# Two-expert attention kernel: block 0's softmax weights in PSUM, the first weights in halves on two load queues, the last copy in two, and a new issue order

## The chip, the cores and the metric

The kernel runs on one core of one Trainium2 chip. TensorE (PE, with its weight loads as PEld), VectorE (DVE), ScalarE (ACT) and GpSimd (POOL) work side by side, and SyncE (SP) issues DMAs and forwards semaphores. The metric is device microseconds of one execution, the median of repeated runs; lower is better.

## The reference, cut to what matters

```python
x_unf = x_pad[:, idx, :]                     # 2 x 4096 tokens, 7 taps, 192 = 8 heads x 24
w = softmax(weight_gen)                      # over the 7 taps, per head and token
x = einsum('bshk,bskhg->bshg', w, x_unf)     # attention
h = x @ w1_in;  g = h / (1 + exp(-h));  x = g @ w1_out            # expert 1, d_ff 2048
h = x @ w2_in;  g = P(h) / (Q(h) + 1e-6);  out = g @ w2_out       # expert 2
# P is a cubic, Q = 1 + |b0| |h| + |b1| h^2; all in float32
```

## The kernel before, in words

The 8192 tokens are cut into 16 blocks of 512 (4 tokens on each of 128 partitions). For each block the kernel computes the attention, turns the result so that features lie on partitions, and runs expert 1 and then expert 2, each in 8 units of 256 hidden features. Every float32 product is made of a high and a low part (`xh`, `xl`; `wa` high, low; `wb`; `g1h`, `g1l`; `g2h`, `g2l`), and TensorE works as two row groups of 64 rows that run side by side. All 9,728 products of 512 columns go through line 808. Eight PSUM areas are used: banks A to D (`h`, the turned tiles, decoded weights) and the accumulators of the two experts.

Nothing is scheduled at run time. `ORDER` is a list of some 3,960 names, written by a search outside the kernel, and each engine issues its instructions in the order in which the names stand there. A name is an operation, a unit and a block: `M2.0` is operation `M` of column 2 in block 0. A letter behind a colon is the buffer or bank taken, `@1` the second engine of the operation's choice, `^` and `^^` a load of the ACT function table, `<2` or `>2` a shift of the two row groups against each other. The names that matter here:

- `s0l`, `s0m`, `s0d`, `s0e`, `s0t`, `s0n`: load of weight_gen for block 0, maximum, subtraction, exponential, sum and reciprocal, and normalisation; `s1` is that of block 1, `s2` to `s5` of the rest.
- `X.b`, `Z.0`: loads of x. `Mj`, `mj`: the products of x and weights for 4 and 3 taps (768 and 576 elements); `pj`, `rj`, `aj`: the additions that leave 576, 384 and 192 of them.
- `q0B0l0`, `q0A0l1`: loads of the halves of an input weight (expert 0, piece B or A, half 0 or 1), `q0O1l0` of an output weight. Each half of B and A of the first expert comes in two DMAs of 64 partitions. Weights lie in HBM with 64 bits a number; `a` (ACT) and `4` (DVE) make a float32 of each half in a PSUM bank, `h` the high part, `x` the low part.
- `W0.0`, `W1.0`: transposes that only keep TensorE busy; `WT.0`, `T.b`: the attention turned; `XH`, `XL`: its high and low part.
- `Au`, `Ku` (expert 1) and `Bu`, `Qu` (expert 2): the products into an `h` bank. `S`, `H`, `L`: SiLU, high and low part; `U`, `V`, `u`, `w`, `Y`, `N`, `G`, `g`, `h`, `l`: the rational function and its parts. `C`, `E`, `I`, `F` and `D`, `P`, `J`, `R`: products into the accumulators. `EC`, `EM`, `EA`: the turn from expert 1 to 2; `FC`, `FT`, `FR`, `FE`, `FA`, `O`: the way out.

An `h` bank is free for its next tenant when `L` (line 923) or `w` (line 973) has read it. The first expert's first unit needs `XH`, `XL`, the weight A of its columns and the weight B.

Of the kernel before, what the change touches and what calls it, by code (L numbers as in the profile page):

```python
# [21 lines left out]
P = 128  # L22
# [28 lines left out]
    S4.0 H4.0:e r2.1 L4.0:t F4.0>2 M1.1:p q1B040:B q0O3h q1B0a1 q0O3x S6.0 A7.0:D>2 q1O0l1:i C2.0>2 q1O1l1:u
    q1O1l0:d r3.1@1 q1A0a0 H6.0:h q1B041 p1.1 q1B0h1 q1A0a1 K7.0 E4.0 S7.0 H7.0:v E5.0 E3.0 C4.0 M0.1:a L6.0:q
    C6.0<2 q1A040:A C7.0<4 p0.1 q1A041 q1B0x1 q1A1l0:c r0.1@1 a0.1:j q1A1l1:m L7.0:r q1O0a0 r1.1@1 a3.1@1 q1O040:D
    q1B0h0 a1.1 q1B0x0 q1O0a1 a2.1 q1A0h F6.0 q1O041 q1A0x q1O0h q1O0x q1O1a0 I6.0 T.1:B q1O140:A s3l:o E7.0 E6.0
    TR.1 XH0.1:q q1O1a1 F7.0 XL0.1:s q1O141 I7.0 I4.0>2 q1A1a0 EC.0:g q1O1h q1A140:B q1O1x A2.1:D q1A1a1 q1A141
    q1O2l1:w K2.1 S2.1 s3m H2.1:c EM.0 L2.1:n q1O2l0:t A1.1:A K1.1 q1A1h q1O3l1:d q1O2a1 S1.1 EA.0 XH1.0:h H1.1:p
    X.2 A0.1:D K0.1 S0.1 H0.1:a q1A1x XL1.0:i s3d@1 q1O2a0 L1.1:x s2n@1 L0.1:g s2s A3.1:B K3.1 S3.1 H3.1:l B0.0:C
    q1O240:A q1O241 B5.0:D q1O2h q1O3a1 L3.1:y Q0.0 V0.0:e q1O2x Q5.0 E1.1:B C3.1 V5.0:b C1.1<2 U5.0:w AW.2 B3.0:A<4
    U0.0:v Y0.0 Y5.0 m1.2:t M1.2:u I2.1<4 F1.1<1 q1O3l0:r Q3.0<1 M0.2:m ^^N0.0 U3.0:j F0.1<1 q1O3a0 V3.0:k m2.2:x
    u5.0 u0.0 w0.0 w5.0 I0.1<1 I1.1>1 B2.0:C>3 q1O340:D u3.0 m0.2:p q1O341 p0.2@1 F2.1>3 F3.1>3 w3.0 Q2.0>3 C0.1>3  # L60
# [1076 lines left out]
```

## Time and profile before

| | |
|---|---|
| median of 3 runs | 1193.26 us (1193.02 to 1193.70) |
| profiled execution | 1195.1 us, of which 1193.3 us lie between its first and last instruction |
| TensorE clock granted | 0.998 of full speed over the span |
| busy | PE 98%, DVE 91%, ACT 88%, POOL 43% |
| DMA | 45.42 MB |

The profile is of one execution. The page has the busy times, the span in slices and the groups of instructions; the trace answers for single stretches (windows, timeline), for waits and for the chain of work that ended last. TensorE's instructions overlap, so its busy share alone doesn't tell whether it ran at its full rate; the number of matmuls in a window does.

### The profile page before, as it was taken

What the parts mean: (1) busy time and instruction counts of PE and PEld (TensorE: products, weight loads), DVE (VectorE), ACT (ScalarE), POOL (GpSimd) and SP (SyncE); (2) the same over time, 40 slices, a digit from 0 to 9 for tenths busy, and PEclk for the clock granted to TensorE, in tenths of its full rate; (3) what the DMA queues carried; (4) which work ended last, traced back from release to release, by engine and by line L of the source; (5) the groups of instructions that cost most, each with busy time, mean ns of one, the idle gap of its engine ahead of it and who ended that gap; (6) DMA issues with size and microseconds to landing.
All of it is one profiled execution on the core that took longest, in us unless ns stands there. A gap on an engine that the chain in (4) does not pass through costs nothing.

```text
span 1193.3 us, 24919 instructions
## 1 busy us (share of the span) xinstructions
PE 1164.3 (98%) x10332; PEld 1072.2 (90%) x10332; DVE 1091.2 (91%) x1016; ACT 1049.3 (88%) x1023; POOL 518.1 (43%) x340
## 2 busy tenths in 40 slices
...
DMA packets 17753, 45.42 MB, mean 38 GB/s; under 512 B 2412, under 2 KB 9194, under 8 KB 17640
## 3 DMA queue, kind: packets, MB, share of 16 engines
...
q14 instruction: 32, 0.26, 0.1%
...
## 4 chain that ended last, share of the span: by engine, by line
PE 84%; DVE 5%; ACT 4%; issue 2%; SPq 0%; DVEq 0%; ACTq 0%
PE acc L808 44%; PE h L808 39%; DVE y L979 1%; ACT h L915 1%; DVE g1l L923 1%; ACT g1h L919 1%; PE to L1028 1%; PE tp L821 1%; DVE t L970 1%; DVE t L990 0%; DVE t L973 0%; DVE g2l L1000 0%; ACT L1102 0%; ACT y L964 0%; ACT t L960 0%
## 5 line engine op out<-in xcount | busy, mean ns | idle before, releaser
L808 PE MATMUL h<-xh,wa 64*128 64x512 f32 x2048 | 433.2, 393 | 6.6 <-DVE t L973 2.7
L808 PEld LDWEIGHTS h<-xh,wa 64*128 64x128 f32 x2048 | 274.7, 184 | 37.2 <-issue 4.9
L808 PE MATMUL h<-xh,wb 64*128 64x512 f32 x1024 | 293.5, 388 | 0.0
L808 PE MATMUL h<-xl,wa 64*128 64x512 f32 x1024 | 293.2, 388 | 0.0
L808 PE MATMUL acc<-g1h,wo 64*128 64x512 f32 x1536 | 286.1, 391 | 0.0
L808 PE MATMUL acc<-g2h,wo 64*128 64x512 f32 x1536 | 282.4, 390 | 0.0
L1000 POOL TENSOR_TENSOR g2l<-t,g2h 128x1024 fp32r<-128x1024 f32 x73 | 188.7, 2594 | 167.5 <-ACT g2h L464 55.0
L808 PEld LDWEIGHTS acc<-g1h,wo 64*128 64x128 f32 x1536 | 209.1, 184 | 11.5 <-ACT g1h L919 0.5
L808 PEld LDWEIGHTS acc<-g2h,wo 64*128 64x128 f32 x1536 | 210.1, 184 | 9.9 <-SPq L404 0.2
L808 PE MATMUL acc<-g2l,wo 64*128 64x512 f32 x1024 | 203.6, 391 | 1.6 <-DVE xl L842 1.5
L808 PE MATMUL acc<-g1l,wo 64*128 64x512 f32 x1024 | 202.9, 391 | 0.6 <-DVE g1l L923 0.4
L741 POOL TENSOR_TENSOR pr<-xw,aw 128x576 f32<-128x576 f32 (+1 forms) x76 | 116.7, 1549 | 172.9 <-PE acc L808 53.8
L979 DVE SCALAR_TENSOR_TENSOR y<-y,b_sb 128x1024 f32<-128x1024 f32 x128 | 177.0, 1389 | 10.4 <-ACT y L964 10.0
L923 DVE TENSOR_TENSOR g1l<-h,g1h 128x1024 fp32r<-128x1024 f32 x128 | 155.4, 1219 | 28.5 <-ACT g1h L919 19.4
L990 DVE SCALAR_TENSOR_TENSOR t<-t,a_sb,y 128x1024 f32<-128x1024 f32 x128 | 173.2, 1363 | 8.4 <-ACT y L987 7.7
L970 DVE TENSOR_TENSOR t<-t,h 128x1024 f32<-128x1024 f32 x128 | 155.1, 1214 | 16.6 <-ACT t L960 8.2
L915 ACT ACTIVATE h<-h 128x1024 f32<-128x1024 f32 x128 | 129.6, 1013 | 44.4 <-PE h L808 42.4
L960 ACT ACTIVATE t<-h,a_sb 128x1024 f32<-128x1024 f32 x128 | 153.7, 1204 | 16.0 <-PE h L808 13.2
L973 DVE SCALAR_TENSOR_TENSOR t<-t,a_sb,h 128x1024 f32<-128x1024 f32 x128 | 163.5, 1279 | 3.9 <-ACT y L964 0.4
L964 ACT ACTIVATE y<-h,b_sb 128x1024 f32<-128x1024 f32 x128 | 141.9, 1113 | 27.7 <-PE h L808 20.5
L808 PEld LDWEIGHTS h<-xl,wa 64*128 64x128 f32 x1024 | 151.1, 184 | 7.4 <-DVE xl L842 0.3
L808 PEld LDWEIGHTS h<-xh,wb 64*128 64x128 f32 x1024 | 150.9, 184 | 7.1
...
## 6 DMA issues: line engine op xcount, KB each, us to landing
...
```

What stands on the lines that cost most here:

```text
L741: e.tensor_tensor(out=p.rearrange("p k (h g) -> p k h g", g=G), in0=st[xw][:, j + k0:j + k0 + n, :].rearrange("p k (h g) -> p k h g", g=G) ...
L808: return pe.matmul(out=out, lhsT=w, rhs=x, start=start, stop=stop)
L821: return lambda: pe.transpose(out=st[tp][:, a, j * P + r * DL:j * P + (r + 1) * DL], in_=columns(a, j, r), identity=ident[HALF[r], HALF[r]],)
L915: act.activation(out=st[hb], in_=st[hb], func=AF.Silu)
L923: dve.tensor_tensor(out=t, in0=st[hb], in1=st[gh].bitcast(F32), op=ALU.subtract)
L960: act.activation(out=q, in_=st[hb], func=AF.Identity, scale=a_sb[:, 3:4], bias=a_sb[:, 2:3])
L964: act.activation(out=q, in_=st[hb], func=AF.Abs, scale=b_sb[:, 1:2])
L970: dve.tensor_tensor(out=st[t], in0=st[t], in1=flat(), op=ALU.mult)
L973: dve.scalar_tensor_tensor(out=st[t], in0=st[t], scalar=a_sb[:, 1:2], in1=flat(), op0=ALU.add, op1=ALU.mult)
L979: dve.scalar_tensor_tensor(out=st[y], in0=st[y], scalar=b_sb[:, 0:1], in1=st[y], op0=ALU.add, op1=ALU.mult)
L990: dve.scalar_tensor_tensor(out=st[t], in0=st[t], scalar=a_sb[:, 0:1], in1=st[y], op0=ALU.add, op1=ALU.mult)
L1000: e.tensor_tensor(out=q, in0=st[t], in1=st[gh].bitcast(F32), op=ALU.subtract)
```

## The change

Four things are changed. Block 0's normalised attention weights are copied by ACT into PSUM bank D (`cw`), and the products of its columns 0 to 2 read them there, on DVE; their last two additions (`r`, `a`) become one reduction over four (`fold`). The first piece of weight A gets its high and low parts in halves of 512 columns (`h0`, `x0`, `h1`, `x1`), and units 0 and 1 ask only for the first half; the second DMA of each half of this piece and of the first B is issued from ACT's queue in place of SP's. The last block's copy out of the accumulator is in two halves, one on ACT and one on DVE. And the whole `ORDER` is a new one: of its 240 lines none is kept, and of them the first and the last are shown.

```diff
--- before
+++ after
 ORDER = """
-    s0l cz:f s0m X.0 q0B0l0:h q0B0l1:x Z.0 s0d ^^s0e s0t s0n@1 M2.0@1:a M1.0@1:l q0B0a0 q0B040:B M0.0@1:q q0B0a1
-    q0B041 q0B0h0 m2.0@1:h m0.0@1:r M3.0@1:u m3.0@1:w q0B0h1 m1.0@1:e p2.0 p0.0 r2.0 p1.0 q0A0l0:b q0A0a0 cn
-    q0A040:C W0.0:A r0.0 r1.0 cl q0A0l1:s q0A0a1 q0A041 p3.0 a0.0@1:g s1l q0O0l0:n q0O0a0 ca r3.0@1 a1.0 q0B0x0 a3.0
-    a2.0 q0A0h q0A0x q0O040:D q0B0x1 s2l:k q0O0l1:d q0O1l0:t q0O0a1 q0O1l1:v WT.0 W1.0:B s1m q0O041 q0A1l0:h q0O1a0
-    q0A1l1:e s2m s1d@1 XH0.0:r XL0.0:y cr s2d@1 q0O140:C q0O1a1 q0O0h q0O0x q0O141 s1e s1t q0O1h@1 s2e X.1 q0O1x
-    A0.0 A1.0:A q0A1a0 K0.0 ^S0.0 H0.0:l L0.0:t q0O2l0:c A2.0:D K1.0 S1.0 H1.0:q s1n@1 L1.0:w K2.0 I0.0:C q0O2l1:x
+    s0l s0m s0d X.0 ^^s0e s0t s0n cw:D cz:f q0B0l0:i M2.0:g M0.0:b q0B0a0 q0B040:B M1.0:l q0B0l1:q cn Z.0 q0B0a1
+    q0B041 q0A0l1:p q0O0l1:r m3.0:q s1l q0A0l0:n q0B0h0 m0.0:w m1.0:h m2.0:o p0.0@1 M3.0:x q0B0x0 a0.0:a p1.0
+    q0O3l1:v s1m p3.0@1 q0B0h1 q0A0a0 W0.0:A q0A0a1 q0O1l0:u a1.0 q0O0l0:s p2.0 r3.0@1 cl a2.0 q0O1l1:e q0A040:C
+    a3.0 q0A1l1:d q0A1l0:b X.1 q0A0h0 ca q0B0x1 s1d@1 q0O0a0 s1e q0A041 q0O0a1 q0O040:D q0O2l0:h WT.0 XH0.0:l q0A0x0
+    q0O041 W1.0:B XL0.0:j q0A0h1 A0.0 K0.0 q0A0x1 q0O1a0 q0O0h q0O0x q1B0l0:t A1.0:A K1.0 q0O1a1 q0O140:C A2.0:D
 ...
-    P4.15 FR.14 R4.15 J4.15 FC.15:u FT.15:D FE.14@1 FA.14 O.14 FR.15 FE1.15 FA1.15 O1.15 FE0.15 FA0.15 O0.15
+    P6.15 P5.15 h4.15@1:p P3.15 l4.15:a D7.15 J7.15 J4.15 R7.15>2 R4.15 FR.14 P7.15 P4.15 D4.15 FE.14@1 FA.14 O.14
+    FC0.15:p FC1.15@1 FT.15:D FR.15 FE0.15 FA0.15 FE1.15@1 FA1.15 O0.15 O1.15
 """
```

```diff
                 f = slice(4 * n * q + 1, 4 * n * (q + 1))
+                queues = (sp, sp if m or c else act)
                 if k == "A" and m:
                     sp.dma_start(out=t[:, 0:4 * n - 1], in_=w_in[m][0:P, f])
...
                     for h in range(2):
-                        sp.dma_start(out=t[R[h], 0:4 * n - 1], in_=w_in[m][h * P:h * P + DL, f])
+                        queues[h].dma_start(out=t[R[h], 0:4 * n - 1], in_=w_in[m][h * P:h * P + DL, f])
                 elif k == "B":
                     for h in range(2):
                         f = slice(4 * n * (i + 2 * h) + 1, 4 * n * (i + 2 * h + 1))
-                        sp.dma_start(out=t[R[h], 0:4 * n - 1], in_=w_in[m][P if m else DL:D if m else P, f])
+                        queues[h].dma_start(out=t[R[h], 0:4 * n - 1], in_=w_in[m][P if m else DL:D if m else P, f])
                 else:
                     sp.dma_start(
...

-        def hi(e):
-            w, a, _ = halves()
-            if e is act:
-                act.activation(out=a, in_=w, func=AF.Copy, scale=256.0)
-            else:
-                dve.tensor_scalar(out=a, in0=w, scalar1=256.0, scalar2=None, op0=ALU.mult)
+        def hi(i=None):
+            q = slice(None) if i is None else slice(512 * i, 512 * (i + 1))
+
+            def run(e):
+                w, a, _ = halves()
+                w, a = w[:, q], a[:, q]
+                if e is act:
+                    act.activation(out=a, in_=w, func=AF.Copy, scale=256.0)
+                else:
+                    dve.tensor_scalar(out=a, in0=w, scalar1=256.0, scalar2=None, op0=ALU.mult)
+            return run
+
+        def lo_half(i):
+
+            def run(e):
+                w, a, b = halves()
+                q = slice(512 * i, 512 * (i + 1))
+                less(b[:, q], w[:, q], a[:, q])
+            return run

         def less(out, w, a):
...
             return
-        plan.op(name + "h", 0, "ACT DVE", hi, rd=full, wr=wt)
+        if k == "A" and (m, c) == (0, 0):
+            for i in range(2):
+                wt = [("W", m, k, c, i)]
+                plan.op(f"{name}h{i}", 0, "ACT DVE", hi(i), rd=[full[i], dt[0]], wr=wt)
+                plan.op(f"{name}x{i}", 0, "DVE", lo_half(i), rd=[full[i], dt[0], *wt], wr=wt)
+            return
+        plan.op(name + "h", 0, "ACT DVE", hi(), rd=full, wr=wt)
         plan.op(name + "x", 0, "DVE", lo, rd=[*full, *wt], wr=wt)

...

+        wp = ("h", "w", b)
+
         def weight(j):
-            return st["aw", b][:, j * HK:(j + 1) * HK].rearrange("p (h k) -> p k h", k=K)
+            t = st["aw", b] if b or j == JB - 1 else st[wp].rearrange("p a c -> p (a c)")
+            return t[:, j * HK:(j + 1) * HK].rearrange("p (h k) -> p k h", k=K)
+
+        def copy_w(e):
+            st[wp] = t = bank(wp)
+            act.activation(out=t[:, 0, 0:JB * HK], in_=st["aw", b][:, 0:JB * HK], func=AF.Copy)
+
+        if b == 0:
+            plan.op("cw", b, "ACT", copy_w, rd=[wt], wr=[(*wp, 0)])

         for j in range(JB):
             halves = [(*pr, j, 0), (*pr, j, 1)]
+            near = b == 0 and j < JB - 1

             def mul(i, j=j, halves=halves):
...

+            def fold(e, j=j, halves=halves):
+                if ao not in st:
+                    st[ao] = new(ao, [P, JB, D])
+                dve.tensor_reduce(
+                    out=st[ao][:, j], in_=st[halves[0]].rearrange("p k d -> p d k"), axis=AX.X, op=ALU.add
+                )
+
             pt, qt = [(*halves[0], 0)], [(*halves[1], 0)]
-            plan.op(f"M{j}", b, "POOL DVE", mul(0), rd=[*(xt if j == JB - 1 else xt[:1]), wt], wr=pt)
-            plan.op(f"m{j}", b, "POOL DVE", mul(1), rd=[*xt, wt], wr=qt)
+            who, w = ("DVE", (*wp, 0)) if near else ("POOL DVE", wt)
+            plan.op(f"M{j}", b, who, mul(0), rd=[*(xt if j == JB - 1 else xt[:1]), w], wr=pt)
+            plan.op(f"m{j}", b, who, mul(1), rd=[*xt, w], wr=qt)
             plan.op(f"p{j}", b, "DVE POOL", add0, rd=[*pt, *qt], wr=pt)
+            if near:
+                plan.op(f"a{j}", b, "DVE", fold, rd=[*pt, (*ao, 0)] if j else pt, wr=[(*ao, j)])
+                continue
             plan.op(f"r{j}", b, "DVE POOL", add1, rd=pt, wr=pt)
             plan.op(f"a{j}", b, "POOL DVE", add2, rd=[*pt, (*ao, 0)] if j else pt, wr=[(*ao, j)])
...
         first = [(*hb, 0)] if (m, b, u) == (0, 0, 0) else []
-        rd = [(*xh, 0), (*xl, 0), ("W", m, "A", u // 4), ("W", m, "B", u // 4)]
+        wa = ("W", m, "A", u // 4) if m or u > 3 else ("W", m, "A", 0, u // 2)
+        rd = [(*xh, 0), (*xl, 0), wa, ("W", m, "B", u // 4)]
         plan.op(f"{'AB'[m]}{u}", b, "PE", run(0), rd=[*first, *rd], wr=[(*hb, 0)])
         plan.op(f"{'KQ'[m]}{u}", b, "PE", run(1), rd=[*rd, (*hb, 0)], wr=[(*hb, 0)])
...

+        out = [(*acc, i) for i in range(2 if (m, b) == (1, NB - 1) else 1)]
         for n in range(2):
             for low in range(2):
...
                     name, b, "PE", run(n, low, f"{name}.{b}"),
-                    rd=[((gl if low else gh) + (0,)), ("W", m, "O", u // 2), (*acc, 0)],
+                    rd=[((gl if low else gh) + (0,)), ("W", m, "O", u // 2), *out],
                 )

...

-        def copy(e):
-            st[of] = t = new(of, [P, 2 * BT]).rearrange("p (a c) -> p a c", a=2)
-            round_to(e, t, st[acc])
+        def copy(h):
+
+            def run(e):
+                if of not in st:
+                    st[of] = new(of, [P, 2 * BT]).rearrange("p (a c) -> p a c", a=2)
+                round_to(e, st[of][:, h], st[acc][:, h])
+            return run

         def back(n):
...

-        plan.op("FC", b, "ACT DVE", copy, wr=[(*acc, 0), (*of, 0)])
-        plan.op("FT", b, "PE", back(0), rd=[(*of, 0), ("ident", 0)], wr=[(*tp, 0)])
-        plan.op("FR", b, "PE", back(1), rd=[(*of, 0), ("ident", 0), (*tp, 0)], wr=[(*tp, 0)])
+        if b == NB - 1:
+            whole = [(*of, 0), (*of, 3)]
+            for h in range(2):
+                plan.op(f"FC{h}", b, "ACT DVE", copy(h), wr=[(*acc, h), whole[h]])
+        else:
+            whole = [(*of, 0)]
+            plan.op("FC", b, "ACT DVE", copy(slice(None)), wr=[(*acc, 0), *whole])
+        plan.op("FT", b, "PE", back(0), rd=[*whole, ("ident", 0)], wr=[(*tp, 0)])
+        plan.op("FR", b, "PE", back(1), rd=[*whole, ("ident", 0), (*tp, 0)], wr=[(*tp, 0)])
         if b == NB - 1:
             for h in range(2):
                 f = (*of, 1 + h)
```

## Rows read from the trace of the kernel before

**Rows 1.** Busy time by engine, from part 1 of the page.

```profile
PE 1164.3 (98%) x10332; PEld 1072.2 (90%) x10332; DVE 1091.2 (91%) x1016; ACT 1049.3 (88%) x1023; POOL 518.1 (43%) x340
```

**Rows 2.** Windows: stretch, length, busy time (instructions) by engine, clock, DMA share, GB/s.

```profile
45.00:105.00 60.00, 56.80 (x463) 45.68 (x459) 56.03 (x67) 54.13 (x63) 34.59 (x26) 1.00 0.40 129
...
150.00:300.00 150.00, 150.00 (x1349) 143.05 (x1348) 135.36 (x123) 135.20 (x130) 68.27 (x44) 1.00 0.08 25
300.00:600.00 300.00, 297.98 (x2668) 276.66 (x2667) 277.53 (x249) 269.17 (x256) 138.18 (x89) 1.00 0.09 29
600.00:900.00 300.00, 297.14 (x2660) 268.79 (x2658) 275.66 (x247) 261.36 (x251) 132.16 (x87) 1.00 0.08 27
900.00:1160.00 260.00, 259.21 (x2331) 242.51 (x2329) 241.71 (x215) 235.61 (x227) 94.17 (x56) 1.00 0.06 18
```

**Rows 3.** Timeline of the first 30 us: start, length, engine, line, operation.

```profile
0.74 0.39 SPq L516 DMA_DIRECT2D aw<-in_weight_gen_dram  x1
...
2.92 0.39 DVE L522 TENSOR_REDUCE aw<-aw 128x32 f32<-128x224 f32 x1 [2.92 <-DMA aw<-in_weight_gen_dram]
...
5.35 0.57 POOL L540 TENSOR_TENSOR aw<-aw 128x224 f32<-128x224 f32 x1 [1.57 <-DVE aw L536]
...
6.57 1.83 DVE L741 TENSOR_TENSOR pr<-xw,aw 128x768 f32<-128x768 f32 x2 [1.39 <-POOL ident masks.py:199]
...
8.79 0.77 ACT L602 ACTIVATE tops<-raw 128x512 f16<-128x512 bf16 x1 [4.64 <-DMA raw<-in_moe_w_in_dram]
...
11.36 0.77 ACT L602 ACTIVATE tops<-raw 128x512 f16<-128x512 bf16 x1 [1.79 <-DMA raw<-in_moe_w_in_dram]
12.17 0.70 DVE L615 SCALAR_TENSOR_TENSOR dec<-raw,tops 128x512 int32<-128x512 int32 x1 [1.01 <-ACT tops L602]
...
12.78 3.63 DVE L741 TENSOR_TENSOR pr<-xw,aw 128x576 f32<-128x576 f32 x5
...
16.32 1.42 DVE L751 TENSOR_TENSOR pr<-pr 128x576 f32<-128x576 f32 x2
...
17.66 0.55 DVE L755 TENSOR_TENSOR pr<-pr 128x384 f32<-128x384 f32 x1
...
21.60 0.35 DVE L761 TENSOR_TENSOR ao<-pr 128x192 f32<-128x192 f32 x1
...
23.29 1.21 DVE L636 SCALAR_TENSOR_TENSOR wa<-dec,wa 128x1024 fp32r<-128x1024 f32 x1
...
28.13 1.23 DVE L842 TENSOR_TENSOR xl<-tp,xh 128x1024 fp32r<-128x1024 f32 x1
...
29.41 0.19 PEld L808 LDWEIGHTS h<-xl,wa 64*128 64x128 f32 x2 [0.17 <-DVE b_sb L496]
```

**Rows 4.** Windows again: the DMA engines from 2 to 24 us.

```profile
2.00:24.00 22.00, 11.31 (x80) 11.34 (x81) 16.88 (x28) 8.88 (x14) 4.98 (x9) 1.00 1.04 263
```

**Rows 5.** Groups by line and shape: engine, names, shapes, count, busy time, mean ns.

```profile
L979 DVE SCALAR_TENSOR_TENSOR y<-y,b_sb 128x1024 f32<-128x1024 f32 x128 | 177.0, 1389 | 10.4 <-ACT y L964 10.0
...
L973 DVE SCALAR_TENSOR_TENSOR t<-t,a_sb,h 128x1024 f32<-128x1024 f32 x128 | 163.5, 1279 | 3.9 <-ACT y L964 0.4
...
L522 DVE TENSOR_REDUCE sm<-sm 128x128 f32<-128x896 f32 x3 | 3.2, 1077 | 0.0
...
L522 DVE TENSOR_REDUCE sm<-sm 128x64 f32<-128x448 f32 x1 | 0.6, 614 | 0.0
...
L751 POOL TENSOR_TENSOR pr<-pr 128x576 f32<-128x576 f32 x36 | 54.2, 1510 | 54.7 <-DVE pr L741 45.5 <-ACT h L915 8.2
...
L464 ACT ACTIVATE e<-acc 128x512 f32<-128x512 f32 x12 | 7.1, 589 | 2.5 <-PE acc L808 2.3
```

**Rows 6.** Waits of the matmuls, 100 to 1165 us: total, times, longest.

```profile
PE h L808 <- DVE t L973: 1.9, 3, 0.9
...
PE h L808 <- DVE g1l L923: 1.2, 2, 0.8
```

**Rows 7.** Chain that ended last, from 1180 us: start, length, work.

```profile
1186.66 1.03 ACT of L464
```

More of the change, by code (lines that the diff above doesn't have):

```diff
@@ L51 @@
[L51 to L60, printed above, removed]
@@ new lines @@
+    XH0.2:m XL0.2:o U6.0:y E6.1>2 EC.1:l Y6.0 D0.0>2 P1.0 EM.1 h3.0:h l4.0@1:d A0.2:C J4.0 R1.0>2 u6.0 w6.0 R0.0>2
+    AW.3 K0.2>2 N2.0 D4.0>2 EA.1 s3l:w B7.0:A P4.0 Q7.0 N6.0 G2.0 G6.0 D3.0 XH1.1:k g2.0 h2.0:c XL1.1:s ^S0.2 H0.2:v
+    l2.0:t g6.0 B1.1:B<2 L0.2:q V7.0:r h6.0:f J3.0<2 R4.0 s3m Q1.1 l3.0@1:x U7.0:n U1.1:b V1.1:d u7.0 w7.0 A3.2:C
+    P2.0 s3d@1 K3.2 R3.0 J2.0 S3.2 H3.2:u B2.1:A>2 D2.0>2 P3.0 D6.0 Y7.0 ^^N7.0 G7.0 u1.1 L3.2:i Q2.1<2 U2.1:h
+    M1.3:p V2.1:l l6.0@1:a J6.0<2 w1.1 R2.0 A1.2:B s3e P6.0 B3.1:C g7.0 Y1.1 K1.2 h7.0:e l7.0@1:g ^S1.2 H1.2:t u2.1
@@ new lines @@
+    B6.6:C>2 H7.7:p XL0.8:g E4.7>2 E6.7>2 C5.7>2 Q6.6 s5m L7.7:k F6.7 B7.6:B FT.5:A ^^N4.6 Y5.6 F7.7 FR.5 I7.7
+    U6.6:i Q7.6>2 G4.6 C7.7>2 N5.6 FE.5 u6.6 w6.6 V6.6:t g4.6 E7.7 l3.6:o J3.6:C C6.7>2 D2.6 I6.7<2 U7.6:q Y6.6 FA.5
+    J0.6 V7.6:p Y7.6 A0.8:A>2 D0.6>2 EC.7:r G5.6 P2.6 P0.6 K0.8 N6.6 G6.6 u7.6 w7.6 h1.6@2:l J1.6 R2.6>2 A1.8:B>2
+    EM.7 g5.6 l1.6:e ^S0.8 H0.8:y h4.6@1:c h5.6:k l5.6@1:h O.5 X.9 D1.6>2 EA.7 XH1.7:u P1.6 D3.6 L0.8:r K1.8<2
+    XL1.7:l R0.6<2 J2.6<2 S1.8 B0.7:A B2.7:D R5.6 R3.6 g6.6 h6.6:x ^^N7.6 l4.6@1:m R1.6 Q0.7 J5.6 R4.6>2 Q2.7>2 G7.6
```

446 lines of the change are left out of this document (223 added, 223 removed).

## The prediction

> **What bounds the kernel now.** I read the busy times first. TensorE is busy 98% of the span, and no other engine is above 91% [rows 1], so a gain must be time in which TensorE has nothing to do, or works below its best rate. The windows tell how much there is. In the best long stretch, 150 to 300 us, 1349 matmuls take 150 us, or 8.99 per us. From 300 to 600 and from 600 to 900 us the counts are 2668 and 2660 where that rate would give 2698: 30 and 38 missing, or 3.3 and 4.2 us. From 45 to 105 us it is 463 in place of 540, or 8.5 us, while DVE and ACT are busy for 93% and 90% of the stretch [rows 2]: there the weights of both experts are still being decoded. The reader is to see three places: the start; the stretch up to 105 us; and small losses over the long middle.
>
> Next I read the start. DVE joins the second half of weight B at 12.17 us, after ACT had waited for that load until 11.36 us, and from there it works almost without a gap until `XL` ends at 28.13 + 1.23 = 29.36 us. The weights for the first products with `xl` are loaded 0.05 us later, at 29.41 us [rows 3]. Up to there TensorE has next to nothing to multiply. So DVE's list of work, shifted by the arrival of B, sets the start. The DMA engines are full the whole time, at a share of 1.04 and 263 GB/s [rows 4]. Of the middle I read the waits: the products into an `h` bank wait 1.9 and 1.2 us, in five waits, behind lines 973 and 923, which are the last readers of the bank's tenant before [rows 6]. At the end the chain holds one copy of 1.03 us on ACT after the last product [rows 7].
>
> **The start, step by step.** *Weights in PSUM.* `cw` stands between `s0n` and the first `M`. `s0n` ended at 5.92 us and the first `M` began at 6.57 us [rows 3], when x had come. A copy of 512 elements takes ACT 0.59 us [rows 5], this one has 224, and it ends by 6.51 us: I take 0, and up to 0.6 if x should come earlier. *Loads on ACT.* ACT works in order, so the second DMA of B's half 0 stands behind `cw`, and that of half 1 behind `q0B0a0`, which waits for half 0. What is queued behind them is `q0B0a1`, and DVE's `q0B041` waits for it, with `m0`, `m1` and `m2` after it. A load of 112 KB was used 2.18 us after its issue (0.74 to 2.92 us) [rows 3]; without its 0.43 us at 263 GB/s [rows 4] that is 1.75 us of delay, and 256 KB at half of that rate, shared with SP's loads, are 1.95 us: 3.7 us in all. So half 0 is there at 5.9 + 3.7 = 9.6 us (before 8.79), half 1 at 13.3 us, and `q0B041` starts 0.8 us of `a1` later, at 14.1 us: 1.9 us later than before. The bounds are 0, if ACT's loads come as early as SP's did, and 3.8 us, if they get a third of the rate. What SP saves in issue time is hidden by the full DMA engines. *DVE's list between `q0B041` and the end of `XL`.* Gone are `M3` and `m3` (two of the five in 3.63 us: 1.45), `p0` and `p3` (1.42), three `r` (1.65), `a0` (0.35), `s2m` (0.61, the reduction of 448) and half of `q0A0x` (0.60): 6.1 us [rows 3, 5]. New are three reductions of 768 elements, between 0.61 us for 448 and 1.08 us for 896 [rows 5], so 0.94 each, 2.8 us. The sum is 3.3 us less. *POOL beside DVE.* Column 3 and `p0` are now six instructions on POOL; at 1.51 us at most [rows 5] they take 9 us after `q0B041`, and end about when DVE has its `a2`, so they are not last. But `p1`, `p2` and the join `q0A040` on DVE read two SBUF operands while POOL runs. Line 979, with two such operands, takes 1.389 us on average, line 973, with one in PSUM, 1.279 us [rows 5]; POOL is busy 43% of the span [rows 1], so one beside a POOL that never rests costs 0.11 / 0.43 = 0.26 us. I take three of these, 0.8 us; the bounds are 0 and three whole POOL additions, 4.5 us.
>
> The Trainium skill, "SBUF — State Buffer", section "SBUF: two separate sides", says that a DVE instruction with two SBUF inputs and a POOL instruction exclude each other for their whole length. By it the three would cost up to 4.5 us and not 0.8, and the sum below would be 3.7 us more; the means of the two lines have its sign but not its size.
>
> The start: 1.9 - 3.3 + 0.8 = -0.6 us, between -3.3 and +5.0.
>
> **The stretch up to 105 us.** The lists have the same work for DVE from `XL0.0` to `XL1.0` within half a microsecond, so DVE gives nothing more. But counted in products per row group, 154 stand ahead of `XL0.1` where 148 did, and 172 ahead of `L2.1` where 163 did: 6 to 9 products that TensorE does earlier, at 2 / 8.99 = 0.22 us each, so 1.3 to 2.0 us. I take -1.5; the bounds are -4 (half of the 8.5 us lost there) and +1.
>
> **The middle.** From the second block on I counted in both lists how many products stand between the instruction that makes an operand and the first product that reads it. With none between there are 26 groups of products before and 17 after; with at most 8 per row group, 106 and 83. That is the room ahead of products. The same count for a bank (none or at most two products between its last reader and its next tenant) rises from 57 to 71 of 290. So one sort of wait gets rarer and the other, which is the one that rows 6 show most of, gets more frequent. ACT has 83 table loads in place of 89, but ACT isn't the bound. The 9,008 matmuls from 150 to 1160 us would take 8.3 us less at the best stretch's rate, and 5.9 us more at that of 600 to 900 us [rows 2]: these are the bounds. I take -1.5, a fifth of the 7.5 us that 300 to 900 us lose.
>
> **The end.** `FC0` on ACT and `FC1` on DVE run together: 0.59 us [rows 5] in place of 1.03 [rows 7], so -0.4; between -0.4 and +0.5 if the new last products end less evenly.
>
> **Sum.** -0.6 - 1.5 - 1.5 - 0.4 = -4.0 us. The profiled execution took 1195.1 us, 1.8 us of them outside its span, and would take 1191.1. The median of the runs was 1193.26 us, 1.8 us below the profiled one; the sum is taken off it: 1189.3 us.
>
> **Rivals.** *No change: POOL holds DVE.* If `p1`, `p2` and `q0A040` each wait for a whole POOL addition, the start is 4.5 - 0.8 = 3.7 us later: 1193.0 us. For it speaks that POOL works without a pause just then; against it, the small difference of lines 979 and 973. It is what the Trainium skill's rule of the section above would make of it. *No change: the loads on ACT.* At 3.8 in place of 1.9 us, and with nothing gained in the stretch behind a later start, the time is 1189.3 + 1.9 + 1.5 = 1192.7 us. For it speaks that the DMA engines were full already; against it, that DVE has 3.3 us less to do. *Slower: the banks.* The first products into an `h` bank wait more often for `L` or `w`. At the rate of 600 to 900 us the middle is 5.9 us longer: 1193.26 - 0.6 - 1.5 + 5.9 - 0.4 = 1196.7 us. One such wait was 3.1 / 5 = 0.62 us [rows 6], so it decides from about eight more of them on (start, stretch and end give 2.5, and 2.4 more is what can be told from no change). For it speaks the count of 71 against 57; against it, that of the 290 handovers of before only five made a matmul wait long enough to be named there. *More than forecast.* The halves come as early as before and the middle comes half-way to the best rate: 1193.26 - 2.5 - 1.5 - 4.0 - 0.4 = 1184.9 us.
>
> **How the numbers follow.** A difference of 0.2% (2.4 us) is about what a measurement of this kernel can tell from no change. The forecast, a gain of 2.4 to 6 us, has a chance of 0.37; more than that 0.15; no change by POOL 0.12, by the loads or otherwise 0.15; slower, by the banks above all, 0.21. So faster has 0.52, within 0.2% 0.27, slower 0.21. The range leaves out the ends of the second and of the last case, about a tenth each: 1184.5 to 1196.5 us. The forecast's own is 1187 to 1191.
>
> **What would show it.** In the new profile `q0B041` (line of the join, 512 elements, second) starts near 14 us, and near 12 if ACT's place costs nothing. `XL0.0` ends near 28.8 us, and `M` on DVE takes the 0.92 us of before. The joins and `p` on DVE near 20 us are longer than 0.7 us if POOL holds them. The window from 45 to 105 us has some 475 matmuls, those from 300 to 600 and 600 to 900 us some 2675. The waits behind lines 973 and 923 come to 3 us, or over 8 if the banks decide. The prediction is wrong if `XL` ends after 31 us, or if the windows of the middle differ from before by more than 30 matmuls each.

## The result: slower, and where the profile after shows it

The changed kernel takes 1200.74 us (median of 6 runs, 1198.07 to 1205.18), the kernel before 1193.07 beside it: a ratio of 1.0069, with a 95% interval of 1.0049 to 1.009. By the ratio that is 8.2 us more (by the two medians 7.7) where 4 less were forecast. It lies outside the forecast range. The profiled run is the longest of the six, 1205.18 us with a span of 1203.4, so its sums come out some 4 us above the median.

The busy times (part 1 of the page), then the windows with the columns of [rows 2]. The window from 26 to 37 us is new here.

```profile
PE 1168.5 (97%) x10332; PEld 1030.7 (86%) x10332; DVE 1083.0 (90%) x1013; ACT 1040.5 (86%) x1019; POOL 522.1 (43%) x342
```

```profile
26.00:37.00 11.00, 7.57 (x34) 6.07 (x36) 10.77 (x16) 6.79 (x12) 2.53 (x5) 0.53 0.71 196
...
45.00:105.00 60.00, 55.33 (x457) 43.35 (x457) 56.57 (x69) 54.15 (x65) 33.16 (x26) 1.00 0.43 131
...
150.00:300.00 150.00, 148.91 (x1334) 134.27 (x1332) 142.31 (x125) 135.67 (x130) 71.88 (x46) 1.00 0.09 28
300.00:600.00 300.00, 298.15 (x2686) 264.01 (x2684) 270.48 (x245) 268.94 (x258) 138.35 (x89) 1.00 0.10 29
600.00:900.00 300.00, 295.50 (x2628) 263.27 (x2626) 266.31 (x240) 258.97 (x248) 133.81 (x86) 0.99 0.09 27
900.00:1160.00 260.00, 260.00 (x2344) 231.50 (x2342) 236.87 (x220) 228.83 (x221) 92.02 (x58) 1.00 0.07 20
```

Two things differ from [rows 2]. From 600 to 900 us 32 matmuls are missing against before (2628 for 2660) and 15 from 150 to 300, while 18 are gained from 300 to 600 and 13 from 900 to 1160: the middle is uneven, not worse everywhere. And from 26 to 37 us there are 34 matmuls at a granted clock of 0.53, nearly all at the lower of TensorE's two levels, 1.2 GHz. Now the start, the timeline that answers [rows 3] (ACTq is ACT's queue issuing a DMA):

```profile
5.57 0.36 ACT L757 ACTIVATE h<-aw 128x224 f32<-128x224 f32 x1 [1.55 <-DVE aw L540]
5.59 0.55 ACTq L592 DMA_DIRECT2D raw<-in_moe_w_in_dram  x1
...
12.57 0.78 ACT L603 ACTIVATE tops<-raw 128x512 f16<-128x512 bf16 x1 [6.64 <-DMA raw<-in_moe_w_in_dram]
12.60 0.48 ACTq L592 DMA_DIRECT2D raw<-in_moe_w_in_dram  x1
...
16.88 0.79 ACT L603 ACTIVATE tops<-raw 128x512 f16<-128x512 bf16 x1 [3.53 <-DMA raw<-in_moe_w_in_dram]
...
17.70 0.70 DVE L616 SCALAR_TENSOR_TENSOR dec<-raw,tops 128x512 int32<-128x512 int32 x1 [2.77 <-ACT tops L603]
...
21.72 1.47 DVE L797 TENSOR_REDUCE ao<-pr 128x192 f32<-128x768 f32 x1
...
33.03 1.22 DVE L884 TENSOR_TENSOR xl<-tp,xh 128x1024 fp32r<-128x1024 f32 x1
...
35.90 0.62 PE L850 MATMUL h<-xl,wa 64*128 64x512 f32 x2
```

The reader is to see a staircase. ACT makes the copy `cw`, issues the second DMA of B's half 0 at 5.59 us and then waits for it with `q0B0a0` until 12.57 us; only then, at 12.60 us, can it issue that of half 1, which it uses at 16.88 us. So `q0B041` starts at 17.70 us, 5.5 us later than in [rows 3], and all that DVE has behind it moves with it: `XL0.0` starts at 33.03 us, 4.9 us later, and the first product with `xl` 6.4 us later. Before, SP had issued all four DMAs of B back to back from 3.02 us on (timeline of before):

```profile
3.02 2.48 SPq L591 DMA_DIRECT2D raw<-in_moe_w_in_dram  x4
...
29.52 0.40 PE L808 MATMUL h<-xl,wa 64*128 64x512 f32 x2
```

The waits of the matmuls over the whole span (engine, line, what it waited for, us, times, longest):

```profile
PE h L850 <- DVE xl L884: 3.9, 3, 2.0
PE h L850 <- DVE wo L650: 2.3, 1, 2.3
PE h L850 <- DVE g1l L967: 1.3, 2, 0.9
...
PE h L850 <- DVE t L1017: 0.5, 1, 0.5
```

The same waits before:

```profile
PE acc L808 <- DVE xl L842: 1.5, 1, 1.5
...
PE h L808 <- DVE wo L636: 0.6, 2, 0.5
...
PE h L808 <- DVE xl L842: 0.5, 1, 0.5
```

The waits for an `h` bank that [rows 6] showed (lines 973 and 923, now 1017 and 967) did not grow: 1.8 us in three waits. Two others did, for `xl` (3.9 us, before 2.0) and for `wo` (2.3 us, before 0.6): 6.2 us together in place of 2.6. The end (timeline), beside [rows 7]:

```profile
1196.56 0.60 ACT L464 ACTIVATE of<-acc 128x512 f32<-128x512 f32 x1 [4.42 <-PE acc L850]
1197.18 0.69 DVE L468 COPY of<-acc 128x512 f32<-128x512 f32 x1 [1.18 <-ACT of L464]
```

The last copy starts at 1196.56 us against 1186.66: 9.9 us lost by then. Its two halves don't run together; DVE's begins when ACT's has ended. What makes it wait, the program's dependences or the chip, was not tried.

### The profile page after: what moved, and what is told of

Its sections match the earlier page's. It is cut to its first block, busy times and chain, and to the rows that moved or that the text cites. A ratio compares the mean times of both kernels' runs of the same rounds, so it can differ in the third digit from the quotient of the medians.

```text
span 1203.4 us, 24916 instructions
## 1 busy us (share of the span) xinstructions
PE 1168.5 (97%) x10332; PEld 1030.7 (86%) x10332; DVE 1083.0 (90%) x1013; ACT 1040.5 (86%) x1019; POOL 522.1 (43%) x342
## 4 chain that ended last, share of the span: by engine, by line
PE 53%; DVE 3%; ACT 2%; issue 1%; DMA 0%; POOL 0%; SPq 0%; DVEq 0%; ACTq 0%
PE acc L850 28%; PE h L850 24%; PE to L1076 1%; DVE y L1023 1%; DVE t L1014 0%; PE tp L863 0%; ACT t L1004 0%; DVE t L1017 0%; DMA e<-e 0%; DVE t L1034 0%; DVE xl L884 0%; DVE g1l L967 0%; ACT y L1008 0%; ACT y L1031 0%; ACT h L959 0%
## 5 line engine op out<-in xcount | busy, mean ns | idle before, releaser
L850 PE MATMUL h<-xh,wa 64*128 64x512 f32 x2048 | 424.2, 393 | 8.9 <-DVE xl L884 3.7
L850 PE MATMUL h<-xh,wb 64*128 64x512 f32 x1024 | 287.1, 389 | 0.0
L850 PE MATMUL h<-xl,wa 64*128 64x512 f32 x1024 | 286.4, 389 | 0.2 <-DVE xl L884 0.2
L1044 POOL TENSOR_TENSOR g2l<-t,g2h 128x1024 fp32r<-128x1024 f32 x70 | 180.1, 2581 | 213.5 <-DVE g2h L468 69.6
L850 PEld LDWEIGHTS acc<-g1h,wo 64*128 64x128 f32 x1536 | 203.6, 184 | 19.9 <-DVE g1l L967 1.0
L772 POOL TENSOR_TENSOR pr<-xw,aw 128x576 f32<-128x576 f32 (+1 forms) x85 | 129.5, 1534 | 177.0 <-PE acc L850 75.7
L850 PE MATMUL acc<-g2l,wo 64*128 64x512 f32 x1024 | 193.8, 389 | 0.0
L850 PE MATMUL acc<-g1l,wo 64*128 64x512 f32 x1024 | 193.1, 393 | 0.5 <-DVE g1l L967 0.3
L850 PEld LDWEIGHTS h<-xh,wb 64*128 64x128 f32 x1024 | 142.0, 185 | 12.1
L850 PEld LDWEIGHTS h<-xl,wa 64*128 64x128 f32 x1024 | 141.7, 185 | 12.4 <-DVE xl L884 0.9
```

Source lines behind the costliest of these rows:

```text
L772: e.tensor_tensor(out=p.rearrange("p k (h g) -> p k h g", g=G), in0=st[xw][:, j + k0:j + k0 + n, :].rearrange("p k (h g) -> p k h g", g=G) ...
L850: return pe.matmul(out=out, lhsT=w, rhs=x, start=start, stop=stop)
L1044: e.tensor_tensor(out=q, in0=st[t], in1=st[gh].bitcast(F32), op=ALU.subtract)
```

## Experiments

My theory after the result: most of the loss is the loads on ACT's queue (theory 1), the rest are stalls of the new order. Rivals: the order and its banks make all of it (rival 2); the fold, with POOL beside DVE, sets the start (rival 3); POOL, by holding DVE, makes the loss (rival 4).

| kernel | median us | ratio to before | 95% interval |
|---|---|---|---|
| changed kernel | 1200.74 | 1.0069 | 1.0049 to 1.009 |
| e1, loads on SP | 1198.35 | 1.0028 | 1.0019 to 1.0037 |
| e2, no fold | 1201.09 | 1.0049 | 1.0034 to 1.0064 |
| e3, loads on SP, no fold | 1197.10 | 1.0017 | 1.0008 to 1.0026 |
| e4, before + loads on ACT | 1203.11 | 1.0072 | 1.006 to 1.0084 |
| e5, more warm transposes | 1198.35 | 1.0050 | 1.0036 to 1.0064 |
| e6, loads on SP, weights in SBUF | 1197.24 | 1.0031 | 1.0019 to 1.0043 |
| e7, before + copy in halves | 1194.97 | 1.0014 | 1.0005 to 1.0022 |
| e8, loads on SP, three moves | 1190.72 | 0.9980 | 0.9970 to 0.9990 |
| e9, three moves, loads on ACT | 1196.98 | 1.0027 | 1.0016 to 1.0038 |
| e10, loads on SP, two moves | 1193.15 | 1.0001 | 0.9990 to 1.0011 |
| e11, as e8, no fold | 1189.96 | 0.9970 | 0.9958 to 0.9982 |
| e12, as e8, one last copy | 1191.10 | 0.9983 | 0.9974 to 0.9991 |

e1 to e4, e5 to e8 and e9 to e12 ran with three sets of runs of the kernel before (medians 1194.54, 1193.28 and 1193.34 us), so ratios are compared below. They are worked out from all runs of a set and can differ from the quotient of the medians by up to 0.0008. One thousandth is 1.19 us.

**e1, loads on SP.**

```
-                queues = (sp, sp if m or c else act)
+                queues = (sp, sp)
```

> The changed kernel with all its DMAs issued on SP again; nothing else differs. Theory 1 (the second halves of B stand behind ACT's waits, and the start that they make late is carried to the end): ACT's tops start near 8.8 and 11.4 us, the join of B's second half near 12.2 to 13.4 us in place of 17.70, XL0.0 ends near 29.5 to 31 us in place of 34.25, no half clock before 36 us, the count of products at 45 us rises from 74 to 120 or more, and the time falls by 4 to 5.5 us, to about 1195.5. Rival 2 (the order of the middle and its banks make the loss): the start improves but the time stays above 1198.5. Rival 3 (the fold and POOL beside DVE set the start, and not the loads): the join comes earlier, XL0.0 still ends after 32.5 us, and the time stays above 1198.

The timeline of its start:

```profile
11.85 0.70 DVE L616 SCALAR_TENSOR_TENSOR dec<-raw,tops 128x512 int32<-128x512 int32 x1 [0.60 <-ACT tops L603]
...
12.46 2.07 DVE L772 TENSOR_TENSOR pr<-xw,h 128x576 f32<-128x576 f32 x3
...
27.20 1.22 DVE L884 TENSOR_TENSOR xl<-tp,xh 128x1024 fp32r<-128x1024 f32 x1
```

The join `q0B041` is back at 11.85 us and `XL0.0` ends at 28.42, 0.9 us before that of [rows 3] and earlier than the 29.5 to 31 expected. The window from 26 to 37 us is at full clock. The ratio falls by 0.0041, 4.9 us, as theory 1 said; the median is above the 1195.5 expected, in a set in which the kernel before was 1.5 us slower too. But 0.0028 stays, with a start that is better than before, so something else costs over 3 us, and more in some runs than in others (1195.43 to 1199.58 us; the profiled run is the fastest of the ten, so its trace shows less of the loss than the median has).

**e2, no fold; e3, no fold and loads on SP.** Three `r` and three `a` on DVE stand in place of the reductions, and the lines that make the fold are taken out.

```
-    ... m0.0:w m1.0:h m2.0:o p0.0@1 M3.0:x q0B0x0 a0.0:a p1.0
+    ... m0.0:w m1.0:h m2.0:o p0.0@1 M3.0:x q0B0x0 r0.0 a0.0@1:a p1.0
...
-    ... a1.0 q0O0l0:s p2.0 r3.0@1 cl a2.0 ...
+    ... r1.0 a1.0@1 q0O0l0:s p2.0 r3.0@1 cl r2.0 a2.0@1 ...
```

> The changed kernel with the fold undone: the three reductions of 768 elements (1.47 us each) are again three additions r on DVE (0.55) and additions a, one of them on DVE. Loads stay on two queues, the weights in PSUM. Theory 1: B's join stays at 17.7 us, XL0.0 ends 0.5 to 2 us earlier than 34.25, and the time is about 1199 to 1200.7. Rival 3 (the fold is what delays the start): XL0.0 ends by 31 us and the time falls by 3 us or more.

> Both of the two edits above: all DMAs on SP and the fold undone. What is left of the change is block 0's weights in PSUM, the columns that POOL takes, the last copy in halves and the new order. Theory 1: XL0.0 ends near 28.5 to 30 us and the time is 1192.5 to 1194.5, the kernel before's within 0.15%, so the order of the middle is worth at most 1 us either way. Rival 2: the time stays above 1196 although the start is that of before. If it is below 1191, the order was worth what the prediction gave it and the start hid it.

In e2 `XL0.0` starts at 33.27 us where the changed kernel has 33.03: the three reductions take 4.4 us, and the six additions in their place, two of them beside POOL, 4.9 us. So the fold doesn't make the start late, and my 0.5 to 2 us earlier was wrong. e2's interval and the changed kernel's overlap. e3's ratio is 0.0011 below e1's with intervals that overlap, although its `XL0.0` starts 1.6 us later than e1's (28.79 for 27.20 us): what the fold is worth to the end can't be told from these, and rival 3 falls. e2 and e3 differ by the loads alone: 0.0032, or 3.8 us. e3 misses my 1192.5 to 1194.5, since the rest that e1 left is there too.

**e4, before with the loads on ACT.** The `queues` line of the change, and the two lines that use it, in the kernel before, in its own order.

> The kernel before with one edit: the second DMA of each first B and first A load is issued on ACT. Its order is that of before, in which ACT has less ahead of them. Theory 1 (a DMA that ACT issues stands behind what ACT waits for, here the tops of the first half): the second half of B's second load is issued only after ACT's tops of the first, near 8.5 us or later, B's second join moves from 12.17 to 14 us or later, and the time is 1195 to 1200. Rival (two queues bring the loads earlier, since SP has fewer to issue): the join stays at or before 12.2 us and the time is 1191 to 1193.5.

```profile
12.17 0.69 DVE L616 SCALAR_TENSOR_TENSOR dec<-raw,tops 128x512 int32<-128x512 int32 x1
...
12.90 0.47 ACTq L588 DMA_DIRECT2D raw<-in_moe_w_in_dram  x1
...
18.68 0.47 ACTq L588 DMA_DIRECT2D raw<-in_moe_w_in_dram  x1
...
26.67 0.70 DVE L616 SCALAR_TENSOR_TENSOR dec<-raw,tops 128x512 int32<-128x512 int32 x1 [5.55 <-ACT tops L603]
```

The loss is 8.6 us, above my range, and B is not late at all: in this order ACT issues both DMAs of B at 0.74 us, before it waits for anything. It is A that stands behind ACT's waits; its second halves are issued at 12.90 and 18.68 us, and the join `q0A041` moves from 20.33 us, where the trace of before has it, to 26.67. My expectation had the mechanism and the wrong load. The products start 7.9 us late (36.58 for 28.70 us). The choice of the queue alone, with nothing else of the change, costs as much as the whole change.

**e5, more warm transposes.** `WARM = (84, 16)` becomes `(128, 16)`.

> The changed kernel with 128 in place of 84 warm transposes in the first group, so that TensorE doesn't rest from 22.4 us until the first transposes of x; loads still on two queues. Theory 1 with its addition (the late start also drops the clock, since TensorE runs dry, and the first products are then done at the lower level): no stretch at half clock before 50 us, the first product 0.5 to 2 us before 34.45, 8 to 20 more products by 45 us, and the time 1 to 2 us less than the changed kernel's, near 1199. Rival: the half clock from 26 to 36 us stands although TensorE is busy, or the warm transposes push the first products back; then the time is 1200.7 or more.

```profile
26.00:37.00 11.00, 7.59 (x59) 5.68 (x59) 10.77 (x16) 7.68 (x14) 2.49 (x5) 1.00 0.82 214
```

The window is at full clock, with 59 matmuls where the changed kernel has 34; 26 of them are products (line 850) where it has 12, the others transposes, some of them the added ones, which end at 26.97 us. The first product comes at 33.02 us, 1.4 us earlier. What TensorE did before the drop in the changed kernel: its warm transposes end at 22.4 us, and up to 30.87 us it does eight transposes. The ratio falls by 0.0019, 2.3 us, though the intervals overlap. The mean clock over the span is higher in every run of e5, 0.996 to 0.999, than in the six of the changed kernel, 0.991 to 0.994. The profiled run of e5, the slowest of its six, is at the lower clock once later (0.97 from 45 to 105 us).

**e6, loads on SP and the weights read from SBUF.** `t = st["aw", b]` for block 0 too.

> All DMAs on SP, as before, and block 0's products with the attention weights read them from SBUF instead of PSUM (the copy to PSUM is still made but not read); everything else as in the changed kernel. Port theory (an instruction of DVE with two SBUF operands and one of POOL don't run together): the three m on DVE, 0.69 us each beside POOL with the weights in PSUM, take 1.2 us or more each, XL0.0 ends 1 to 3 us later than with the weights in PSUM, and the time is 0.5 to 3 us above that kernel's 1198.35. Rival (they run together as well from SBUF): the m take at most 0.95 us each and the time is that of the kernel with all loads on SP, within 0.1%.

```profile
12.51 4.31 DVE L772 TENSOR_TENSOR pr<-xw,aw 128x576 f32<-128x576 f32 x3
12.68 1.64 POOL L772 TENSOR_TENSOR pr<-xw,aw 128x576 f32<-128x576 f32 x1 [8.27 <-DVE dec L616]
14.29 1.92 POOL L782 TENSOR_TENSOR pr<-pr 128x576 f32<-128x576 f32 x1
```

The three `m` take 4.31 us in place of e1's 2.07, while POOL works beside them, and `XL0.0` starts 1.4 us later (28.63). In the start the port theory holds: DVE's instruction with two SBUF operands waits for POOL's, the one with an operand in PSUM doesn't. That is the rule of the Trainium skill, "SBUF — State Buffer", section "SBUF: two separate sides", in this kernel's numbers. But the time is e1's (1.0031 and 1.0028): the 1.4 us don't reach the end, against the second half of that theory.

**e7, before with the last copy in halves.** `FC.15:u` becomes `FC0.15:u FC1.15@1`, with the functions of the change.

> The kernel before with one edit: block 15's copy FC in two halves, FC0 on ACT and FC1 on DVE. By my term for the end the copy takes 0.6 us in place of 1.03 and the time falls by 0.4 us, to 1194.1, which a comparison can hardly tell from no change; in the trace the stretch from the last product to the transposes of the output is 0.3 to 0.5 us shorter. Rival: nothing there gets shorter, since the transposes wait for the DVE half.

```profile
1184.82 0.60 ACT L464 ACTIVATE of<-acc 128x512 f32<-128x512 f32 x1 [5.59 <-PE acc L808]
1185.44 0.69 DVE L468 COPY of<-acc 128x512 f32<-128x512 f32 x1 [3.22 <-ACT of L464]
...
1186.05 0.95 DVE L468 COPY of<-to 128x768 f32<-128x768 f32 x1
```

Nothing gets shorter: 1.31 us for the two, one after the other, in place of 1.03. In this order block 14's copy, 0.95 us, stands behind `FC1` on DVE as well, and the span ends 8.4 us after the start of `FC0`, where before it ended 6.6 us after that of `FC` (1186.66 to 1193.3). So the 1.7 us that are lost in time are put down to this order (two profiles, one of each kernel), and for the changed kernel, where block 14's copy comes first, only the 0.3 us carry over.

**e8, loads on SP and three moves.** In e1's trace I looked at TensorE's longest stalls in the middle. At 93 and 706 us (timeline):

```profile
92.25 2.56 DVE L1023 SCALAR_TENSOR_TENSOR y<-y,b_sb 128x1024 f32<-128x1024 f32 x1
...
703.04 2.40 POOL L1044 TENSOR_TENSOR g2l<-t,g2h 128x1024 fp32r<-128x1024 f32 x1 [5.08 <-ACT y L1008]
703.07 3.46 DVE L1023 SCALAR_TENSOR_TENSOR y<-y,b_sb 128x1024 f32<-128x1024 f32 x1 [0.17 <-ACT y L1008]
...
707.58 1.21 DVE L884 TENSOR_TENSOR xl<-acc,xh 128x1024 fp32r<-128x1024 f32 x1
...
708.94 0.46 PE L850 MATMUL h<-xh,wa 64*128 64x512 f32 x1 [2.01 <-DVE xl L884]
```

`Y7.8` begins 0.03 us after POOL's `l5.8` and takes 3.46 us in place of 1.28; `XL1.9`, two instructions behind it on DVE, comes late, and TensorE stands for 2.0 us. The changed kernel has the same at 713 us, and after it 3.4 us at the lower clock. At 93 us `Y5.0` is held in the same way (2.56 us) ahead of the decoding of `wo`, for which TensorE waits 2.3 us. At 778 us it is a DMA:

```profile
770.65 0.60 ACT L464 ACTIVATE e<-acc 128x512 f32<-128x512 f32 x1 [0.29 <-PE acc L850]
...
773.49 1.11 SPq L985 DMA_DIRECT2D e<-e  x2
...
777.64 0.70 DVE L988 TENSOR_TENSOR acc<-acc,e 128x512 f32<-128x512 f32 x1 [2.99 <-DMA e<-e]
```

The data of `EM.10` is ready at 771.25 us and issued at 773.49, since SP works in order too and has a wait ahead of it: line 404 puts an empty instruction on SP that passes a PSUM area from one use to the next when TensorE is through. SP's waits from 764 to 781 us:

```profile
SPq L404 <- PE acc L850: 11.1, 3, 5.5
```

The moves:

```
-    ... q1O340:D q1O341 q1O3h Y5.0 Q2.0<2 I0.1<2 F0.1 F2.1 q1O3x A5.1:D ...
+    ... q1O340:D q1O341 q1O3h Q2.0<2 I0.1<2 F0.1 F2.1 q1O3x Y5.0 A5.1:D ...
...
-    ... P2.8 Y7.8 u7.8 K1.10 l5.8@1:f XH1.9:y J0.8 R3.8>2 N6.8 XL1.9:g R2.8>2 ...
+    ... P2.8 K1.10 l5.8@1:f XH1.9:y J0.8 R3.8>2 N6.8 XL1.9:g Y7.8 u7.8 R2.8>2 ...
...
-    ... EC.10:x G6.9 ... XH0.11:h M0.12:a EM.10 h6.9:c EA.10 ...
+    ... EC.10:x EM.10 G6.9 ... XH0.11:h M0.12:a h6.9:c EA.10 ...
```

> The changed kernel with all DMAs on SP and three moves in the order: Y5.0 behind q1O3x; Y7.8 and u7.8 behind XL1.9; EM.10 right behind EC.10. They are aimed at TensorE's three longest stalls in the middle with the loads on SP: 2.46 us at 93 us and 2.17 us at 706 us, where DVE's Y (two SBUF operands) was held by POOL for 2.56 and 3.46 us, and 1.77 us at 778 us, where the DMAs of e were issued late. Theory (what is left of the loss is a few such stalls and the half clock that some of them bring in some runs): the three stalls shrink below 0.8 us each, no run shows half clock near 706 to 720 us, and the time falls by 2.5 to 5 us from 1198.35, to 1193.5 to 1196. Rival (the order loses in many small places, and the stalls only gather what is lost anyway): the last product stays within 1 us of 1186.4 and the time above 1197.

```profile
706.37 2.40 POOL L1044 TENSOR_TENSOR g2l<-t,g2h 128x1024 fp32r<-128x1024 f32 x1 [5.02 <-ACT y L1008]
707.33 1.23 DVE L884 TENSOR_TENSOR xl<-acc,xh 128x1024 fp32r<-128x1024 f32 x1 [1.09 <-ACT xh L880]
708.47 1.40 DVE L1023 SCALAR_TENSOR_TENSOR y<-y,b_sb 128x1024 f32<-128x1024 f32 x1
...
772.02 0.60 ACT L464 ACTIVATE e<-acc 128x512 f32<-128x512 f32 x1 [0.26 <-PE acc L850]
...
772.65 1.11 SPq L985 DMA_DIRECT2D e<-e  x2
```

```profile
300.00:600.00 300.00, 298.25 (x2689) 265.73 (x2687) 272.27 (x246) 270.34 (x260) 141.63 (x91) 1.00 0.10 29
600.00:900.00 300.00, 299.18 (x2678) 267.37 (x2676) 269.77 (x248) 261.36 (x250) 136.74 (x89) 1.00 0.08 27
```

`XL1.9`, with an operand in PSUM, now runs beside POOL in 1.23 us, `Y` behind it takes 1.40, and the DMAs of `e` leave at once. In e8's trace no wait of a matmul around the three places is longer than 0.6 us. The window from 600 to 900 us has 2678 matmuls (e1: 2641), though e8's profiled run is the slowest of its nine and e1's the fastest of its ten. The ratio falls by 0.0048, 5.7 us, more than the 2.5 to 5 us that I expected, and the kernel is faster than the one before. The rival, many small losses, falls. Whether a lower clock in some of e1's runs is a part of these 5.7 us, as my theory had it, isn't shown: only one run of each is profiled.

**e9, the three moves with the loads on ACT; e10, the two moves of `Y` with the loads on SP.**

> The changed kernel, loads on two queues, with the same three moves in the order (Y5.0; Y7.8 and u7.8; EM.10). If the two causes add (the loads on ACT, worth 5 us, and the stalls of the middle), it takes back what the moves gave with the loads on SP (1198.35 to 1190.72 there, about 5 us by the ratios 1.0028 and 0.998): 1195 to 1197, or 2 to 4 us above the kernel before, with the join of B still near 17.7 us and XL0.0 ending near 34 us. Rival (a late start is caught up once the middle doesn't stall, or the stalls only hurt when the start is early): at most 1 us from the kernel before, or above 1199.

> All DMAs on SP and only the two moves of Y (Y5.0; Y7.8 and u7.8); EM.10 stays where the changed kernel has it. Port theory (Y held by POOL makes most of the loss in the middle): most of the gain of the three moves is kept, and the time is 1191 to 1193.5, with the stall near 778 us still 1.5 to 2.4 us. Rival (the late DMAs of e make the larger part): 1195 or more.

e9 gains 0.0042 on the changed kernel and stays 0.0047 above e8: the two causes add within the noise. In e10 `XL` still makes TensorE wait 1.8 us near 779 us; the moves of `Y` give 0.0027 (3.2 us) and that of `EM.10` another 0.0021 (2.5 us), so neither is the larger part by far (e10's and e8's intervals touch); e10's median is at the upper end of what I expected. Rival 4 is thus right in part: what POOL's hold on `Y` costs is the 0.0027, and not the whole.

**e11, e8 without the fold; e12, e8 with one last copy.**

> The three moves, all DMAs on SP, and the fold undone (three r on DVE and additions a). If the fold's three reductions of 1.47 us against six additions are worth nothing to the end, the time is that of the kernel with the three moves, within 1 us: 1190 to 1192. If it saves the 2 us that my prediction counted for it at 0.94 us each, it is 1192.5 or more; if its real price of 1.47 us costs time, 1189.5 or less.

> The three moves, all DMAs on SP, and block 15's last copy undivided on ACT again. In the profiles the two halves ran one after the other (0.60 us on ACT, then 0.69 us on DVE), not together. So the stretch from the start of the last copy to the last addition on DVE should be 0.1 to 0.4 us shorter than the 4.04 us of the kernel with the three moves, and the time the same within 0.1%, 1190 to 1191.5. By my prediction's term it would be 0.4 us longer.

e11 is the fastest kernel of all, 0.9970, but its interval and e8's overlap: no pair of runs shows what the fold is worth, surely not the 2 us I counted. All three pairs lean the same way, though: without it the ratio is lower by 0.0020 (e2), 0.0011 (e3) and 0.0010 (e11), which hints, and doesn't show, that the fold costs about a microsecond rather than saves one. In e12 it is 3.81 us from the start of the last copy to the last addition (1183.35 to 1187.16), in e8 4.04: undivided is 0.2 us shorter, and the times agree.

## Why the prediction was wrong, step by step

I forecast 1189.3 us; it is 1200.74. Two signs that I had named for being wrong came: `XL` ends at 34.25 us, after 31, and from 600 to 900 us the matmuls differ by more than 30. The steps that failed are the price of the loads on ACT (1.9 us in the sum, 5.5 measured), DVE's list (2.5 us less with POOL's share, 0.6 less measured), and the middle, where the sum had a gain and the order brought stalls that no term and no rival had. Slower had a chance of 0.21, but by way of the banks, and they were not it.

**Loads on ACT: the mechanism was right, the size was not.** I wrote that half 1 stands behind `q0B0a0`, and put `q0B041` at 14.1 us with a bound of 3.8 us of delay; it was 17.70, 5.5 us of delay. The step that failed is the price of one load, 3.7 us from issue to use, built on the first small DMA of [rows 3], which was issued before any other. The first took 6.98 us (5.59 to 12.57), the second 4.28. The DMA issues of the kernel before from 2 to 13 us had the right price (names, queue, count, KB each, median us to landing):

```profile
raw<-in_moe_w_in_dram SPq DMA_DIRECT2D x8, 255.9 KB, 6.9
```

SP issued the four of B back to back, so 6.9 us was paid about once; on ACT the second waits until the first is used, and a load's time is paid twice. With 6.9 us for both the sum would have put the join at 20.3 us (5.6 + 6.9 + 6.9 for the loads, 0.9 for `a1`), with the measured 6.98 and 4.28 it is what was seen. A second queue brought no more data: 213 GB/s over the first 26 us, 238 before, though part of that is the late issue (e1, with one queue, has 240). That agrees with the Trainium skill, "Trainium Kernel Development and Optimization", section "Key Constraints", which says that queues of several engines share the same DMA engines and save issue time alone. I had said that this saving is hidden, and still priced the loads as if they were cheap. The rival "the loads on ACT" had the place, and gave 1192.7, for the same reason.

**What the late start set off.** TensorE's clock was no term of my sum. With little to do from 22.4 us on it was at the lower level from 26 to 36 us, just when the first products came; e5 puts that at about 2 us (its interval and the changed kernel's overlap). The other kernels with late loads have it too: from 26 to 37 us the granted clock is 0.53 in e4 and 0.59 in e9.

**DVE's list.** A reduction of 768 elements took 1.47 us, not the 0.94 I put between 448 (0.61) and 896 (1.08) contiguous ones [rows 5]; three cost 1.6 us more than I counted. `p2` took 1.35 us beside POOL, `q0A040` 1.06, so my 0.8 us for POOL was near. The weights in PSUM, which I priced at 0 as a copy, are worth 2.24 us to the three `m` (e6); I had not counted that, because I took POOL's share from the means of lines 979 and 973, where most instructions don't meet POOL at all. The trace of before had the size as well, not the sign alone: of line 979 it gives the shortest, the median and the longest as 1271, 1280 and 3460 ns:

```profile
L979 DVE SCALAR_TENSOR_TENSOR y<-y,b_sb x128: 1271/1280/3460, 84.3 to 1176.4; 128x1024 f32<-128x1024 f32 x128
```

That `XL0.0` ends at 28.4 us in e1, where I had said 28.8, is luck: the 28.8 had 1.9 us for ACT's queue in it, which e1 doesn't use, and without them my terms give 26.9. From `q0B041` to the end of `XL0.0` it is 17.19 us before, 16.57 in e1 and 16.55 in the changed kernel: 0.6 us less, not 2.5.

**The stretch up to 105 us.** It has 457 matmuls, not 475, with the decoding of `wo` held by `Y5.0`. In e8 it has 456. But single profiles differ by more than my 6 to 9 products: other profiles with this order have from 441 (e5) to 480 (e2) there. So this term is neither shown nor refuted.

**The middle.** The banks did not decide, as forecast: 1.8 us of waits behind the two lines. From 300 to 600 us I said some 2675 matmuls and 2686 came. From 600 to 900 us I said the same and 2628 came; my counts of room ahead of products take each instruction as if it started when its turn comes, and saw neither POOL holding `Y` nor SP holding `EM`. With three moves the window has 2678. The gain that the counts promised is there too: from 300 to 600 us the kernels with the new order have 2685 to 2702 matmuls, each in one profile, those with the old one 2664 to 2670 (before, e4, e7). Against that, from 150 to 300 us they have 1324 to 1343, and the old order 1347 to 1351. Over the four windows from 150 to 1160 us e8 has 9033 for 9008 before, so without the stalls -1.5 us for the middle was not too large; the changed kernel has 8992.

**The end.** I had -0.4 us for halves that run together; they run one after the other, and it is 0.2 to 0.3 us more.

By the experiments the 0.0069 are the loads on ACT, 0.0041 to 0.0047 (0.0032 in the pair without the fold), and the stalls that the three moves take away, 0.0042 to 0.0048, less a gain of 0.002 that the rest of the change brings (e8). What stays open: which part brings that gain (the counts from 300 to 600 us point to the order; weight A in halves was not tried by itself), and why 1.4 to 1.6 us at the start (e6 and e3 against e1) don't reach the end while 5 us do.
